# Nine more products of zeros on TensorE at the head of an attention and MLP kernel

## The chip, the cores and the metric

The kernel runs on one core of one Trainium2 chip. The time is device microseconds of one execution. Times before the change: 242.74, 243.67 and 244.24 us, median 243.67. One further execution was taken by the profiler; it is the one that the profile and the trace describe.

## The reference: what is computed

Four batches, eight heads, 768 rows, 64 columns a head. A small matrix of 8 x 8 for each batch and head, sort_net, is balanced by five rounds of softmax over rows and normalisation over columns. It then mixes the eight blocks of 96 rows of k and of v. Attention runs within blocks of 96 rows with the mixed keys and values, and a two-layer network with h * cos(h) follows.

```python
P = sort_net
for _ in range(5):
    P = np.exp(P - np.max(P, axis=-1, keepdims=True))
    P = P / (np.sum(P, axis=-1, keepdims=True) + 1e-09)
    P = P / (np.sum(P, axis=-2, keepdims=True) + 1e-09)
k_sorted = np.einsum('bhij,bhjcd->bhicd', P, k_b)
v_sorted = np.einsum('bhij,bhjcd->bhicd', P, v_b)
scores = scale * np.matmul(q_b, k_sb.transpose(0, 1, 2, 4, 3))
attn = softmax(scores)                  # rows of 96
x = np.matmul(attn, v_sb)               # then 3072 tokens x 512
h = x @ w_in                            # 512 -> 2048
out = (h * np.cos(h)) @ w_out           # 2048 -> 512
```

## The kernel before

The order of all work is written out by hand: each engine runs its instructions in the order in which the calls stand in the source, and waits where one needs another's result. Matrix inputs are converted to bf16 as they are loaded by POOL's DMA queue (q, k and v of batch 0 first, then w_in, w_out and the rest).

The tokens are cut into eight chunks n of four blocks (384 tokens), two chunks a batch. For a chunk the steps are: q transposed (q_turn, L301), scores qk (L422 for chunk 0, L427 for the others), row maximum and subtraction on VectorE (DVE; L482, L488), exp on ScalarE (ACT; L506), transposed p (p_transpose, L532, or a DMA), the product with v (av, L545) and its division (L552, L554), the transpose into xT (L572), then up (L585, cosine on ACT at L589, product on DVE at L592) and down (L609), and the store. The sorted keys come from ks (L360), the sorted values from vs (L450, L460). The parts of one chunk's attention are placed by hand between the up and down products of the chunk before; for chunk 0 there is no chunk before, so its attention stands alone, and its up runs in halves of two blocks: up(0, 0) to up(0, 7), first for the first two blocks.

The head of the kernel is this. POOL issues the loads of q, k and v of batch 0. DVE clears a tile `warm` of 128 x 128 zeros (L209). keep_warm(8) then gives TensorE (PE) eight products of that tile with a column of it, read 512 times; the result goes to a tile `idle` that nobody reads, and no engine waits for it. After that comes the balancing, which the code does for two groups g of two batches: maximum and exp (L240, L241), row sums through a product with a matrix of sums, sk (L262), and four rounds of exp on ACT (L331), sk on PE (L262), reciprocal, product and reciprocal on DVE (L350, L323, L326). PE's place between the rounds is filled: keep_warm(2) and keep_warm(3) after the first two sk, and the 32 transposes of q for chunk 0 (L301) in the later ones. In the second round a one-column copy on POOL, held (L346), waits for the balancing, and three loads of w_in (load_w_in, L158) are issued behind it. The balancing ends with spread(0), which writes bd (L282); the sorted keys of batch 0 (k_sort_0, L360, copied by DVE and ACT into kTs), a turn of bd (v_turn, L436), and the permutation of v on POOL (v_permute, L177, held behind bd by L354) follow. The second group's last step is done later, at L323 to L282 from last_balance().

The filler's own code, with the lines that follow it:

```python
def keep_warm(times):
    idle = big.tile([128, 512], FP32, name="idle", tag="big")
    for _ in range(times):
        nc.tensor.matmul(
            idle[:], warm[:], warm[:, :1].to_broadcast([128, 512]), start=True, stop=True)

keep_warm(8)
```

The rounds of the balancing:

```python
for it in range(4):
    for g in range(NG):
        nc.scalar.activation(E[g], T[g], AF.Exp, scale=ci[g][:])
    ...
    sk = [product(same, E[g]) for g in range(NG)]
    ...
    keep_warm(3 if it == 0 else 0)
```

Of the kernel before, what the change touches and what calls it, by code (L numbers as in the profile page):

```python
# [18 lines left out]
def kernel(  # L19
# [196 lines left out]
# [4 lines that stand above are left out]
            nc.tensor.matmul(  # L220
                idle[:], warm[:], warm[:, :1].to_broadcast([128, 512]), start=True, stop=True)

    keep_warm(8)


    E_eps = [const.tile([128, nb + 1], FP32, name=f"E{g}") for g in range(NG)]
# [717 lines left out]
```

## Time and profile before

| what | value |
|---|---|
| runs | 242.74, 243.67, 244.24 us |
| profiled execution, span from first to last instruction | 242.3 us |
| profiled execution, its time outside the span | not shown on the page |
| PE busy | 232.8 us (96%) |
| DVE, ACT, POOL busy | 173.7, 157.6, 88.2 us |
| chain that ended last | PE 83%, ACT 7%, DVE 4%, DMA 3% |
| of it, products of zeros L220 | 2.4% |
| HBM read, written | 27.27, 6.29 MB |

Times in the profile are microseconds from the start of the span. A row of the timeline gives start, duration, engine, line, operation, result and operands, shapes, the count of merged instructions, and in brackets the idle time ahead and what ended it. PE is the product, PEld the loading of the weights, which runs ahead of the products. A row of the chain gives start, duration and the engine's work to which that stretch of the end-to-end chain is put down. A row of the windows view gives a stretch, its length, the busy time (and instructions) of PE, PEld, DVE, ACT and POOL in it, the granted clock of PE, the share of the DMA engines and GB/s. Matmuls are pipelined and their ends are modelled, so a merged group of PE rows ends some time after its last product has been issued.

### The profile page before, as it was taken

What the parts mean: (1) busy time and instruction counts of PE and PEld (TensorE: products, weight loads), DVE (VectorE), ACT (ScalarE), POOL (GpSimd) and SP (SyncE); (2) the same over time, 40 slices, a digit from 0 to 9 for tenths busy, and PEclk for the clock granted to TensorE, in tenths of its full rate; (3) what the DMA queues carried; (4) which work ended last, traced back from release to release, by engine and by line L of the source; (5) the groups of instructions that cost most, each with busy time, mean ns of one, the idle gap of its engine ahead of it and who ended that gap; (6) DMA issues with size and microseconds to landing.
All of it is one profiled execution on the core that took longest, in us unless ns stands there. A gap on an engine that the chain in (4) does not pass through costs nothing.

```text
span 242.3 us, 5366 instructions
## 1 busy us (share of the span) xinstructions
PE 232.8 (96%) x2163; PEld 149.2 (62%) x2163; DVE 173.7 (72%) x320; ACT 157.6 (65%) x226; POOL 88.2 (36%) x110
## 2 busy tenths in 40 slices
PE   8979899899999999999999999999999999999994
PEld 3869798655666566655666556655565556456553
DVE  6469768996478965986669986898789769635700
ACT  4378866577488974889568957684568376737511
POOL 6469974399880899010535301700000000000000
PEclk9999999999999999999999999999999999999999
DMA  4999999991999958756789858914582460271012
GB/s 50 235 189 176 182 205 231 196 208 54 155 170 192 128 149 85 142 112 164 133 97 138 77 120 181 180 24 107 115 202 60 91 190 0 49 138 43 1 46 87
DMA packets 66681, 30.90 MB, mean 128 GB/s; under 512 B 55392, under 2 KB 62176, under 8 KB 66400
## 3 DMA queue, kind: packets, MB, share of 16 engines
q0 software_dynamic: 24048, 13.64, 40.8%
q1 hardware_dynamic: 42096, 16.72, 29.0%
q8 instruction: 17, 0.28, 0.5%
q10 hardware_dynamic: 512, 0.20, 0.3%
q14 instruction: 8, 0.07, 0.1%
HBM read 27.27 MB, written 6.29 MB: 139 GB/s over the span
## 4 chain that ended last, share of the span: by engine, by line
PE 83%; ACT 7%; DVE 4%; DMA 3%; issue 1%; ACTq 0%; DVEq 0%
PE h L585 33%; PE o L609 28%; PE sc L427 4%; PE av L545 3%; PE ks L360 3%; PE idle L220 2%; DMA vperm<-p_buf 2%; ACT p_buf L506 2%; PE xps L572 2%; PE sk L262 2%; PE vs L460 2%; DVE gg L592 1%; PE vs L450 1%; ACT kTs L288 1%; ACT vS L288 1%; PE pps L532 1%
## 5 line engine op out<-in xcount | busy, mean ns | idle before, releaser
L585 PE MATMUL h<-xT,w_in_t 128*128 128x384 bf16 (+1 forms) x576 | 93.0, 313 | 0.3 <-DVE gg L592 0.2
L609 PE MATMUL o<-w_out_t,gg 128*128 128x512 bf16 x368 | 88.3, 379 | 0.5 <-DVE s L488 0.5
L589 ACT ACTIVATE c<-h,half_pi 128x768 f32<-128x768 f32 (+1 forms) x72 | 59.8, 830 | 28.8 <-PE h L585 26.6
L592 DVE TENSOR_TENSOR gg<-c,h 128x768 bf16<-128x768 f32 (+1 forms) x72 | 61.2, 860 | 22.6 <-ACT c L589 22.6
L585 PEld LDWEIGHTS <-w_in_t 128*128 128x128 bf16 x576 | 53.8, 100 | 27.4 <-issue 1.0
L609 PEld LDWEIGHTS <-gg 128*128 128x128 bf16 x368 | 33.2, 98 | 31.9 <-DVE s L488 0.7
L482 DVE TENSOR_REDUCE mx<-sc 96x4 f32<-96x384 f32 (+1 forms) x43 | 31.9, 743 | 2.9 <-PE sc L427 1.7
L488 DVE TENSOR_TENSOR s<-sc,mx 96x384 f32<-96x384 f32 (+1 forms) x43 | 32.2, 749 | 2.3
L177 POOL COPY vperm<-kv 64x1536 bf16<-64x1536 bf16 (+1 forms) x10 | 28.0, 2837 | 12.1 <-DMA kv<-in_v_dram 12.1
L506 ACT ACTIVATE p_buf<-s 96x768 bf16<-96x768 f32 x32 | 25.9, 839 | 0.5 <-DVE s L488 0.2
L554 DVE TENSOR_TENSOR xn<-av,r 96x512 bf16<-96x512 f32 x32 | 22.0, 686 | 1.1
L427 PE MATMUL sc<-kTs,q_turned 128*128 128x96 bf16 x224 | 16.1, 206 | 0.7 <-DVE s L488 0.7
L134 POOL DMA_DIRECT2D kv<-in_q_dram x24 | 16.0, 688 | 0.7 <-issue 0.7
L552 DVE RECIPROCAL r<-av 96x8 f32<-96x8 f32 x32 | 6.4, 199 | 13.6 <-PE av L545 13.4
L427 PEld LDWEIGHTS <-q_turned 128*128 128x128 bf16 x224 | 12.9, 98 | 5.1 <-DVE s L488 1.3
L288 ACT COPY o_s<-o 128x512 f32<-128x512 f32 (+2 forms) x11 | 5.9, 538 | 15.4 <-PE o L609 9.1
L288 ACT CAST kTs<-ks 128x512 bf16<-128x512 f32 (+2 forms) x25 | 12.4, 497 | 4.8 <-PE ks L360 4.7
L288 ACT COPY kv<-o 128x512 f32<-128x512 f32 x8 | 4.7, 583 | 12.6 <-PE o L609 12.6
L134 POOL DMA_DIRECT2D q_mem<-in_q_dram x16 | 10.7, 685 | 0.3 <-issue 0.3
L589 ACT ACT_TABLE_LOAD x8 | 10.3, 1283 | 0.1
L288 ACT CAST pair<-vs 96x512 bf16<-96x512 f32 (+1 forms) x12 | 8.7, 729 | 2.0 <-PE vs L460 2.0
L288 ACT COPY xT<-xps 128x384 bf16<-128x384 bf16 (+1 forms) x9 | 4.6, 513 | 8.1 <-PE xps L572 8.1
(102 smaller groups left out, 226.7 us busy)
## 6 DMA issues: line engine op xcount, KB each, us to landing
out_dram<-kv SPq DMA_DIRECT2D x12, 256.0 KB, 3.0
out_dram<-o_s SPq DMA_DIRECT2D x11, 256.0 KB, 2.4
w_in_t<-in_moe_w_in_dram POOLq DMA_DIRECT2D x4, 512.0 KB, 10.5
w_out_t<-in_moe_w_out_dram POOLq DMA_DIRECT2D x4, 512.0 KB, 12.8
kv<-in_k_dram POOLq DMA_DIRECT2D x2, 768.0 KB, 13.4
kv<-in_v_dram POOLq DMA_DIRECT2D x2, 768.0 KB, 15.2
pair<-in_k_dram POOLq DMA_DIRECT2D x2, 768.0 KB, 11.7
kv<-in_v_dram POOLq DMA_DIRECT2D x6, 256.0 KB, 7.4
```

What stands on the lines that cost most here:

```text
L134: nc.gpsimd.dma_start(out=q_heads[:, i, :, e], in_=src[:, ih * IC + i, :, e])
L177: nc.gpsimd.tensor_copy(dst, src)
L288: eng.copy(dst, src)
L427: nc.tensor.matmul(out, q_of(n, hp)[:, x:x + 128], keys_of(n, u, h2, hp), start=True, stop=True)
L482: nc.vector.reduce_max(mx[:], scv, axis=AX.X)
L488: nc.vector.tensor_tensor(s, scv, mx.to_broadcast(list(s.shape)), op=ALU.subtract)
L506: nc.scalar.activation(p[:, :, :blk], s_t.pop((n, u)).rearrange("p e h c -> p (e h) c"), AF.Exp, scale=scale)
L554: nc.vector.tensor_tensor(xn.rearrange("p h e d -> p e h d"), avv[:, :, :, :D], r.to_broadcast([blk, 2, H2, D]), op=ALU.mult)
L585: nc.tensor.matmul(h[:, f2, :w], w_in_t[:, kk, f * 128:(f + 1) * 128], xT[n][:, kk, lo:hi], start=(kk == 0), stop=(kk == KC - 1))
L589: nc.scalar.activation(c[:, :, :w], h[:, :, :w], AF.Sin, bias=half_pi[:, 0:1])
L592: nc.vector.tensor_tensor(gt[n, fp][:, :, lo:hi], c[:, :, :w], h[:, :, :w], op=ALU.mult)
L609: nc.tensor.matmul(o[:], gt[n, f // 2][:, f % 2, ts * 128:(ts + 1) * 128], w_out_t[:, f, :], start=(f == 0), stop=(f == FC - 1))
```

## The change

The first call of keep_warm gives PE seventeen products of zeros in place of eight. The calls with two and three stay. On PE nine weight loads and nine products are added ahead of the first sk (L262); the instructions of the other engines and their order stay as they are.

```diff
@@ -220,7 +220,7 @@
             nc.tensor.matmul(
                 idle[:], warm[:], warm[:, :1].to_broadcast([128, 512]), start=True, stop=True)
 
-    keep_warm(8)
+    keep_warm(17)
```

## The prediction

> **What bounds the kernel now.** I read the page first: TensorE (PE) is busy 96% of the span, and its clock line shows full speed in every slice. That line is not to be taken at its word, so I went on to the chain of work that ended last, in order of time, where one form of instruction can be compared early and late.
>
> ```profile
> 1.04 3.60 PE idle L220 x8
> ...
> 27.77 0.50 PE xps L572 x4
> 28.27 0.64 PE pps L532 x8
> 28.92 1.36 PE h L585 x8
> 30.28 0.64 PE pps L532 x8
> 30.92 1.28 PE h L585 x8
> 32.20 0.47 PE av L545 x8
> 32.66 1.21 PE h L585 x8
> 33.87 0.89 PE ks L360 x32
> 34.76 0.36 PE av L545 x8
> 35.12 0.66 PE h L585 x8
> ...
> 79.84 1.73 PE o L609 x8
> ```
>
> Eight products h with 192 columns take 1.28 us at 30.92 and 1.21 at 32.66, but 0.66 us at 35.12; av falls from 0.47 to 0.36. So PE runs at half speed for the first 33 to 34 us and at full speed from there on. The windows view (clock: the figure before the last two) does not say it for the early stretch, but it does know a fall at the very end:
>
> ```profile
> 18.30:23.40 5.10, 5.10 (x80) 4.90 (x77) 5.00 (x6) 4.08 (x8) 5.10 (x6) 1.00 1.13 172
> 238.40:241.80 3.40, 0.32 (x3) 0.04 (x1) 0.29 (x1) 0.27 (x1) 0.00 (x0) 1.00 0.23 71
> 241.80:242.30 0.50, 0.00 (x0) 0.00 (x0) 0.00 (x0) 0.00 (x0) 0.00 (x0) 0.58 0.00 0
> ```
>
> The record evidently begins with its first switch. The last two rows show the clock falling to a mean of 0.58 over the last half microsecond; at half speed that is a fall at 241.9, 3.2 us after the last product (PE's 0.32 us from 238.40 on).
>
> What brought full speed? The chain shows PE going from product to product with no gap from 27.77 (each start is the start before plus its time) until the switch, some 6.0 us. The 3.60 us of zero products at the start did not do it.
>
> **The change, part by part.** Nine products and their weight loads are added on PE ahead of L262. Nothing else moves: every other engine keeps its order.
>
> (a) The zero products. At half speed each takes 0.427 us (3.4 us from the first to the first sk, by eight); at full speed one with 512 columns takes 1.73 / 8 = 0.216 us. Seventeen at half speed would be 7.26 us, until 8.30. The unknown is when PE switches: not before 3.6 us of products and, by the stretch from 27.77, at the latest after about 6.0 us, so between 4.64 and 7.1. I take the middle, 5.9: 11.4 products until then, 5.6 more at 0.216 us, end at 7.1. The ends give 6.5 and 7.7. The first sk starts at 4.43 now, so the balancing begins 2.7 us later (2.0 to 3.3).
>
> [...]
>
> (b) The balancing, from the first sk at 4.43 to bd's end at 13.43, 9.0 us.
>
> ```profile
> 4.43 1.03 PE L262 MATMUL sk<-maskj,L 128*128 128x8 f32 x4
> 5.85 1.03 PEld L262 LDWEIGHTS sk<-E,same 128*128 128x128 f32 x4 [0.44 <-ACT E L331]
> 6.12 0.86 PE L262 MATMUL sk<-E,same 128*128 128x8 f32 x4
> 7.73 1.10 PEld L262 LDWEIGHTS sk<-E,same 128*128 128x128 f32 x4 [0.37 <-ACT E L331]
> 8.06 0.86 PE L262 MATMUL sk<-E,same 128*128 128x8 f32 x4
> 9.67 1.21 PE L262 MATMUL sk<-E,same 128*128 128x8 f32 x4
> 10.30 0.21 DVE L350 RECIPROCAL rr<-sk 128x8 f32<-128x8 f32 x1 [0.47 <-PE sk L262]
> 13.08 0.35 DVE L282 SCALAR_TENSOR_TENSOR bd<-maskp,ci,T 128x128 bf16<-128x128 f32 x1
> ```
>
> Most of a round is DVE and ACT and stays. PE's part shrinks in two ways. The fillers (L220, and the transposes L301) now hold up sk: at 5.85 and 7.73 the weights load, and the product starts 0.27 and 0.33 us later, behind the fillers; at full speed two or three fillers take 0.43 or 0.65 us and are out of the way. That is 0.6 us. And the wait from sk's start to rr (9.67 to 10.30, about 0.6 us) comes five times; no row shows this fp32 form at full speed, so its gain lies between nothing and half, 0.3; I take 0.2, for h's products gain a third to a half: 1.0 us. Together 1.6 (0.6 to 2.1): bd ends 1.1 us later than now.
>
> (c) From bd to the first row maximum, 4.9 us.
>
> ```profile
> 13.48 0.58 PE L360 MATMUL ks<-bd,kv 64*128 64x32 bf16 x16 [0.37 <-DVE bd L282]
> 37.50 0.56 PE L360 MATMUL ks<-bd,kv 64*128 64x32 bf16 x16
> 8.85 0.85 PE L301 MATMUL qps<-ident,q_mem 96*64 96x96 bf16 x12
> 38.76 0.56 PE L301 MATMUL qps<-ident,q_mem 96*64 96x96 bf16 x16
> 17.77 0.80 PE L422 MATMUL sc<-kTs,q_turned 64*96 64x96 bf16 x15 [0.17 <-ACT kTs L288]
> 18.29 0.95 DVE L482 TENSOR_REDUCE mx<-sc 96x8 f32<-96x768 f32 x1 [1.21 <-PE sc L422]
> ```
>
> The key products with 32 columns gain nothing (0.58 and 0.56), the ACT and DVE copies of kTs stay; the scores with 96 columns gain about as the q transposes do (0.85 for twelve, 0.56 for sixteen), 0.25 us on the way to mx, and the end of the key products and of the turn of bd, each waited for once, perhaps 0.15. The maximum starts 0.7 us later than now.
>
> (d) 18.29 to 28.9: nothing. In the row 18.30:23.40 above DVE (the third busy time) works 5.00 of 5.10 us: it goes from maximum to subtraction without a pause, so a faster PE only waits for it. Only the last x transpose gains 0.15 us: up(0, 0) comes 0.5 us later.
>
> (e) The first halves of up(0), to the fifth of them.
>
> ```profile
> 28.81 1.28 ACT L589 ACT_TABLE_LOAD   x1
> 30.32 0.58 ACT L589 ACTIVATE c<-h,half_pi 128x384 f32<-128x384 f32 x1 [0.22 <-PE h L585]
> 30.95 0.80 ACT L288 COPY pT<-pps 96x768 bf16<-96x768 bf16 x1
> 31.99 0.67 PE L545 MATMUL av<-vS,pT 96*128 96x65 bf16 x8
> 35.80 1.60 PE L585 MATMUL h<-xT,w_in_t 128*128 128x192 bf16 x16
> ```
>
> PE alone would save 0.7 on each of three h, 0.25 on each pps, 0.1 on av: over 2.5 us. But av(0, 2) stands in PE's order behind the copy pT, and that behind the table load and the first cosine on ACT, which do not shrink: 1.28 + 0.58 + 0.80 us after the start. So av comes 0.25 us later instead of 0.5. From 31.99 to 35.80, 3.8 us, PE is the bound; at full speed av 0.36, h 0.66, ks 0.89, av 0.36 and h 0.66 are 2.9 us. The fifth up starts 0.25 - 0.9, some 0.7 us earlier; pieces that overlap (ks behind h) take it to 0.9. After it both kernels run at full speed, so this stays.
>
> Sum: +2.7 - 1.6 - 0.4 - 0.15 - 1.4 = -0.85, I take -0.9 us. The span becomes 241.4. The page gives the span alone, 242.3; the runs have a median of 243.67, 1.4 above, and spread over 1.5 us, so I subtract from the median: 242.8. Own range from the bounds of (a), 0.7 either way, and (b), -0.5 to +1.0: 241.6 to 243.8.
>
> Queues. POOL's hold at 7.73 sits in the balancing, so three loads of w_in are issued some 2 us later.
>
> ```profile
> 7.85 2.30 POOL L158 DMA_DIRECT2D w_in_t<-in_moe_w_in_dram  x3
> 14.58 5.48 POOL L177 COPY vperm<-kv 64x1536 bf16<-64x1536 bf16 x2 [0.81 <-DMA kv<-in_v_dram]
> w_in_t<-in_moe_w_in_dram POOLq DMA_DIRECT2D x4, 512.0 KB, 10.5
> ```
>
> That costs nothing: k and v are still landing until 14.58 on the same queue, and w_in, some 10.5 us after its issue, is read from 28.9 on. The permutation of v now waits for that load and not for bd, and starts 0.6 us later behind the later bd; its first reader comes later by as much. If this cover were gone, its 0.6 us would be what remains of (c).
>
> **The rivals.** (1) Full speed does not come or does not hold through the balancing: slower. For it speaks that PE counts as busy for all 5.10 us from 18.30 to 23.40 without a switch, and that the balancing is thin work, with L262 waiting on ACT each round. Against it: those 5.1 us are products with 64 rows only, the zero products are full ones without a gap, and after 34 us nothing but a rest of 3.2 us brought the clock down. If it never rises, 9 x 0.427 = 3.84 us stand ahead of the balancing and nothing on the chain waits for a load to absorb them: 247.5. If it falls again early in the balancing, (a) costs 2.7, (b) returns half, 0.8: 245.6. The point that decides: (a) grows by half of any lateness of the switch, so at a switch 1.8 us later, about 7.7, gain and loss are even.
>
> [...] The rows at 8.85 and 38.76 show transposes to run faster at full speed, not whether they hold it.
>
> (2) The gain is larger: switch at 4.64, the fp32 products at half their time, PE bound in (e) throughout: -0.7 - 0.5 - 0.6 more, down to 241.0. Against it the ACT rows of (e).
>
> (3) The gain is covered: ACT and DVE, not PE, also set the rate after 32 us, and (e) returns 0.5 instead of 1.4; no change, 243.7 to 244.5.
>
> **How the numbers follow.** Forecast 0.55 (242.8, own range 241.6 to 243.8), rival 1 0.20 (half at 245.6, half at 247.5), rival 2 0.12, rival 3 0.13. One per cent, 2.4 us, is about what a measurement of this kernel can tell from no change. Faster by over that: 0.15, most of rival 2 and the edge of the forecast. Slower: 0.17, rival 1 and a little of rival 3. Within: 0.68. The range 241.0 to 245.6 leaves out the worse half of rival 1 and tails.
>
> **What would show it.** After: the starts of L220 change from 0.43 to 0.22 us apart between 4.6 and 7.1; the first sk near 7.1; bd near 14.5; mx near 19.0; eight products h in some 0.7 us from the first on; the fifth up near 34.9. I am wrong if eight h still take 1.3 us, if sk starts after 8, or if up(0, 0) comes as early as 28.9.

## The result, and the profile after

The changed kernel is slower: 245.25 us median of 20 executions against 243.4 us of the kernel before, ratio 1.006 with a 95% interval of 1.0038 to 1.0082 (the ratio leaves disturbed executions out, the medians do not). The forecast was 242.8, faster by 0.4%. The profiled execution took 245.65 us with a span of 243.9 from first to last instruction, 1.6 us longer than the span before.

The clock line of the page, the same that read 9 in every slice before:

```profile
PEclk9955569999999999999999999999999999999999
```

Since the record begins with its first switch, this line now tells what it could not tell before: PE was at full speed early, and then fell back for some 24 us. The windows view, with the clock third from the right:

```profile
1.19:4.60 3.41, 3.41 (x9) 1.21 (x8) 2.19 (x12) 2.30 (x7) 3.41 (x8) 1.00 0.27 20
4.60:8.01 3.41, 3.22 (x19) 1.73 (x17) 1.24 (x11) 0.57 (x2) 0.09 (x1) 1.00 1.30 213
8.01:11.43 3.42, 2.63 (x24) 1.67 (x24) 2.19 (x17) 1.20 (x4) 2.24 (x4) 1.00 1.02 216
11.43:14.84 3.41, 3.04 (x38) 2.79 (x39) 1.90 (x13) 1.91 (x4) 0.38 (x2) 0.50 0.95 186
31.91:35.32 3.41, 3.41 (x39) 2.98 (x37) 1.90 (x4) 1.70 (x4) 2.74 (x2) 0.50 1.24 205
35.32:38.73 3.41, 3.41 (x68) 3.16 (x65) 2.72 (x7) 2.48 (x6) 1.59 (x4) 1.00 1.29 229
```

The 1.00 of the first row means only that the record has not begun: the products of zeros are 0.43 us apart there. The clock rose at 4.60, fell at 11.43 and rose again at 35.32, and these times lie on one grid of 3.413 us (two steps, then seven). It was not an accident of this execution: all twenty have a mean clock between 0.939 and 0.958.

The profiled execution of the kernel before, on the other hand, is not typical of it. 63 further executions of the kernel before were timed beside the experiments, with the mean clock of each. 45 of them have a mean of 0.944 to 0.958, as the changed kernel has; 17 have 0.998 to 1.000, as the profiled one (0.999); one has 0.986. In the changed kernel a mean of 0.950 is a rise in the head, a fall, and 24 us at half speed. Without any zeros at the head (an experiment below) none of twelve executions has a mean under 0.986. So, by their mean clock, eight zeros, too, raised the clock in 45 of the 63 executions, and it fell again; no trace of such an execution was kept. The median of the 45 is 243.25 us, that of the 17 is 244.39. Against the 45 the changed kernel takes 2.0 us more, and nine products at 0.216 us are 1.94: it pays for nine more products and gets back only what most executions had already. The places compared below come from one execution of the rarer kind.

The chain of work that ended last shows what that did.

```profile
1.04 5.60 PE idle L220 x17
7.26 0.31 ACT E L331
7.62 0.40 PE sk L262 x2
...
14.12 0.36 DVE bd L282
...
28.86 0.50 PE xps L572 x4
29.36 0.64 PE pps L532 x8
30.00 1.37 PE h L585 x8
...
33.75 1.28 PE h L585 x8
35.03 0.92 PE ks L360 x32
35.95 0.36 PE av L545 x8
36.32 0.66 PE h L585 x8
```

The first sk of a round now follows the exp on ACT directly (7.57 to 7.62) and takes 0.40 us; before, it waited for the fillers. But h of the first half again takes 1.37 and 1.28 us for eight products, as before, and 0.66 only from 36.32. In the timeline the five places of the prediction's sum stand at:

```profile
6.48 0.51 PE L262 MATMUL sk<-maskj,L 128*128 128x8 f32 x4
...
14.12 0.35 DVE L282 SCALAR_TENSOR_TENSOR bd<-maskp,ci,T 128x128 bf16<-128x128 f32 x1
...
19.34 0.95 DVE L482 TENSOR_REDUCE mx<-sc 96x8 f32<-96x768 f32 x1 [1.22 <-PE sc L422]
...
29.93 1.44 PE L585 MATMUL h<-xT,w_in_t 128*128 128x192 bf16 x8
...
36.99 1.58 PE L585 MATMUL h<-xT,w_in_t 128*128 128x192 bf16 x16
```

The first up of the kernel before:

```profile
28.84 1.44 PE L585 MATMUL h<-xT,w_in_t 128*128 128x192 bf16 x8
```

| place | before | after | later by |
|---|---|---|---|
| first sk | 4.43 | 6.48 | 2.05 |
| bd | 13.08 | 14.12 | 1.04 |
| first row maximum | 18.29 | 19.34 | 1.05 |
| first up | 28.84 | 29.93 | 1.09 |
| fifth up | 35.80 | 36.99 | 1.19 |
| end of span | 242.3 | 243.9 | 1.6 |

Against the profiled execution before, the balancing returns 1.0 of 2.05 us; after it nothing is returned. The lateness then stays at 1.15 to 1.2 us to 190 us. The last 0.4 us comes at 195. The chain of the kernel before goes there from down to up without a wait; that of the changed kernel has a transposing transfer of x between, which landed later. First before, then after:

```profile
194.34 0.86 PE o L609 x4
195.21 3.90 PE h L585 x24
```
```profile
192.14 4.31 DMA xT<-xn
196.59 4.06 PE h L585 x24
```

### The profile page after: what moved, and what is told of

Its sections match the earlier page's. It is cut to its first block, busy times and chain, and to the rows that moved or that the text cites. A ratio compares the mean times of both kernels' runs of the same rounds, so it can differ in the third digit from the quotient of the medians.

```text
span 243.9 us, 5384 instructions
## 1 busy us (share of the span) xinstructions
PE 233.2 (96%) x2172; PEld 148.4 (61%) x2172; DVE 173.8 (71%) x320; ACT 157.6 (65%) x226; POOL 88.0 (36%) x110
## 4 chain that ended last, share of the span: by engine, by line
PE 79%; ACT 7%; DVE 6%; DMA 5%; issue 1%; DVEq 0%; ACTq 0%
PE h L585 33%; PE o L609 26%; PE sc L427 3%; PE av L545 3%; PE ks L360 3%; PE idle L220 2%; DMA vperm<-p_buf 2%; DMA xT<-xn 2%; ACT p_buf L506 2%; PE xps L572 2%; PE vs L460 2%; DVE gg L592 1%; PE vs L450 1%; ACT kTs L288 1%; ACT vS L288 1%
## 5 line engine op out<-in xcount | busy, mean ns | idle before, releaser
L552 DVE RECIPROCAL r<-av 96x8 f32<-96x8 f32 x32 | 6.4, 199 | 13.7 <-PE av L545 13.5
```

## The experiments

Two theories stood against each other. A: the clock rises through the zeros but falls in the thin rounds of the balancing, and so the rest of chunk 0 up to the fifth up runs at half speed as before; had it held, the gain would have come. B: the clock behind the head is worth nothing, since ACT and DVE set the rate there, and the loss is only the later start.

**Fillers in the rounds.** Edit, beside seventeen at the head:

```diff
-        keep_warm(3 if it == 0 else 0)
+        keep_warm((5, 3, 3, 3)[it])
```

> Seventeen products of zeros as in the changed kernel, and more fillers in the balancing: 5, 3, 3, 3 products of zeros behind the four sk in place of 3, 0, 0, 0. Theory A (the clock rises during the seventeen products, but falls back in the thin rounds of the balancing, and the rest of chunk 0 runs at half speed again): the clock holds past the point where it fell, 11.4 us, to the end of the balancing; bd comes some 0.5 us earlier than the 14.1 us of the changed kernel; then it falls in the thin stretch of the sorted keys; time some 0.5 us under the changed kernel, about 244.7. Theory B (the clock after the head is worth nothing, because ACT and DVE set the rate; the loss is only the later start): the added fillers bring nothing, 245.2 or up to 0.5 more.

Measured: 245.34 us, ratio 1.0061 (1.0033 to 1.0088).

```profile
13.28:16.70 3.42, 3.25 (x54) 2.23 (x53) 1.85 (x11) 2.29 (x5) 1.32 (x2) 1.00 1.01 163
16.70:20.11 3.41, 1.95 (x46) 1.64 (x43) 2.35 (x8) 2.92 (x9) 3.41 (x2) 1.00 1.24 208
20.11:23.52 3.41, 3.41 (x51) 3.32 (x47) 3.34 (x4) 2.58 (x6) 3.41 (x5) 0.50 0.88 122
```

The clock held through the balancing and fell at 20.1, behind the sorted keys, in whose stretch the fall had been forecast. That the fall hangs on how much PE has to do is borne out: PE was busy 3.25 of 3.42 us in the step before 16.70, at whose end the clock held, and 1.95 of 3.41 in the next, at whose end it fell. In this execution the clock rose only at 6.46, so the first sk came at 7.39 and bd at 14.88, 0.8 us later than in the changed kernel and not 0.5 earlier. The time did not drop: full speed in the last half of the balancing alone brought nothing more (first sk to bd 7.49 us, against 7.64 in the changed kernel), and the last fillers held up the first sorted keys by 0.3 us (0.71 us from bd to ks, before 0.40).

**Fillers everywhere.** Edit, shortened, beside the last one, where `fill` gives PE products of zeros into the tile named:

```diff
+        fill(ps.rearrange("p t m -> p (t m)"), 2)     # k_sort_0
+        if b == 0: fill(ps.rearrange("p t n -> p (t n)"), 1)     # v_sort_b
+        if n == 0: fill(sc[:, 0], 1)     # qk_part
+        if (n, u) in ((0, 0), (0, 1)): fill(a[:, 0], 2)     # av
```

> As the run before, and fillers in chunk 0 as well, each written into a PSUM tile ahead of its real products: 2 ahead of each group of sorted keys, 1 ahead of each group of sorted values and of each group of scores, 2 ahead of the first two products with v. Theory A: full speed holds from the head up to the first up, eight products h take 0.66 us from the first on, and the time falls below the kernel before: 242.5 (241.8 to 243.4). Theory B: full speed changes nothing and the fillers are in the way: 245.3 to 246.5. If the clock falls all the same, 246 to 248, since each filler then takes 0.43 us.

Measured: 256.42 us, ratio 1.0483 (1.0428 to 1.0538). A miss for both: the clock held to 25.4 us, but each filler stood between the release of a PSUM tile and its real products, and the stretch from bd to the first up grew from 15.8 to 23.3 us. Its total says nothing on the worth of the clock.

**No zeros at the head.** Edit: the first keep_warm is left out.

> No products of zeros at the head at all. Theory A: the eight of the kernel before ended just when the first sk was ready, and did not raise the clock, so this is the kernel before, 243.4 within 0.4 us. Theory B: the same. A third case: without the eight the clock rises later than 33.7 us, or the rounds run slower: 0.5 to 1.5 us more.

Measured: 244.98 us, ratio 1.0036 (1.0002 to 1.007). In its profile the first sk starts at 4.59, when DVE's L is there, and the first up at 29.09, both 0.2 us later than with eight; the fifth up is 0.2 us earlier. So the eight hide behind DVE. What they bring is the rise: the mean clock of these twelve executions is 0.986 to 1.000, and their median of 244.98 us lies nearer to the 244.39 than to the 243.25 above, that is to those executions of the kernel before whose clock did not rise in the head either. The rest of its profiled span, 1.7 us over the kernel before, was lost at 84.65 to 87.94 in a wait for a transposing transfer of p; whether the missing zeros have to do with that wait stays open.

**Thirty-four.** Edit: keep_warm(34).

> Thirty-four products of zeros at the head. Both theories: the seventeen further ones run at full speed, 0.216 us each, so the first sk comes 3.7 us later than in the changed kernel, and nothing downstream takes any of it up: 248.9. If waits on loads behind the balancing take some of it up, 247 to 248.5.

Measured: 251.67 us, ratio 1.0312 (1.0268 to 1.0357).

```profile
0.34:3.76 3.42, 2.72 (x7) 1.01 (x8) 1.61 (x12) 1.49 (x3) 3.05 (x12) 1.00 0.05 4
7.17:10.58 3.41, 3.41 (x19) 1.71 (x17) 0.42 (x6) 0.03 (x1) 0.00 (x0) 1.00 1.08 227
10.58:14.00 3.42, 2.70 (x24) 1.70 (x23) 1.97 (x16) 1.45 (x5) 1.52 (x3) 1.00 0.84 176
14.00:17.41 3.41, 3.35 (x28) 2.98 (x28) 1.85 (x15) 1.59 (x4) 0.91 (x2) 0.50 1.02 143
```

The clock rose at 3.76 already, held as long as the zeros lasted, and fell at 14.00, at the end of the first step in which the balancing stood without them. The first sk came at 9.77, 3.3 us later than with seventeen; the first up was 3.3 us later too: downstream takes nothing up. The rest of the span was lost behind 80 us: against the kernel before the lateness goes from 4.3 to 5.7 us near 90 us and to 7.0 near 120, and at both places the chain waits for a transposing transfer of p, 4.1 and 4.7 us, where that of the kernel before does not.

**Thirteen.** Edit: keep_warm(13).

> Thirteen products at the head and nothing else. Theory A: the clock rises in the same way, the first sk comes 1.4 us later than in the kernel before, the balancing returns 1.0, the clock falls and the rest is as before: 244.0, 1.0 us under the changed kernel, for four products of 0.216 us less. If the clock does not rise with thirteen, 245.5.

Measured: 244.31 us, ratio 1.0013 (0.9971 to 1.0056), not to be told from the kernel before.

```profile
7.95:11.36 3.41, 2.56 (x33) 1.97 (x32) 2.18 (x18) 1.48 (x5) 2.42 (x4) 1.00 1.04 220
11.36:14.78 3.42, 3.14 (x54) 2.78 (x54) 2.05 (x11) 2.05 (x4) 0.28 (x2) 0.50 0.92 180
```

The first sk came 1.14 us later than before and the balancing returned 1.32, so bd stood at 12.90, 0.2 us earlier than before, although the clock fell at 11.36. Four products less than seventeen were worth 1.2 us at bd in these two executions. So the loss of the changed kernel is the part of the zeros that the balancing cannot return. All twelve executions have a mean clock of 0.944 to 0.958, so by it the clock rose in all twelve. Their median is 1.06 us above that of the 45 executions with eight zeros whose clock rose, and five products at 0.216 us are 1.08; the times spread from 242.95 to 251.45 us, so the closeness of the two may be chance.

**Zeros on half the rows.** Edit, beside seventeen at the head:

```diff
-                idle[:], warm[:], warm[:, :1].to_broadcast([128, 512]), start=True, stop=True)
+                idle[:], warm[:64], warm[:64, :1].to_broadcast([64, 512]), start=True, stop=True)
```

> Seventeen products at the head as in the changed kernel, but every product of zeros (those of the fillers in the balancing too) uses only 64 of the 128 rows. In the runs so far, stretches full of products with 64 rows (18 to 25 us) never raised the clock. Theory A (what raises it is the share of the array at work, rows times time, and 64 rows are half): the clock does not rise at the head, all seventeen take 0.43 us, the first sk comes at 8.3 us and nothing is returned in the balancing: 247.3 (246.8 to 248). Theory B (a gapless stretch of any products raises it): as the changed kernel, 245.0, first sk near 6.5.

Measured: 249.68 us, ratio 1.0256 (1.0202 to 1.0311).

```profile
1.04 7.43 PE L220 MATMUL idle<-warm 64*128 64x512 bf16 x17 [1.04 <-DVE warm L209]
8.40 1.02 PE L262 MATMUL sk<-maskj,L 128*128 128x8 f32 x4
9.35 1.03 PE L220 MATMUL idle<-warm 64*128 64x512 bf16 x2
9.50 0.73 ACT L331 ACTIVATE E<-T,ci 128x8 f32<-128x8 f32 x2 [5.21 <-DVE ci L279]
10.31 0.93 PEld L262 LDWEIGHTS sk<-E,same 128*128 128x128 f32 x4 [0.84 <-ACT E L331]
10.31 1.02 PE L262 MATMUL sk<-E,same 128*128 128x8 f32 x4
```

Seventeen products without a gap, 0.425 us apart to the last (it starts at 7.84), and no rise: the first sk came at 8.40 and the clock first rose at 36.96, as theory A has it. It is 2.4 us slower in all than that theory gave; 0.8 of it stands in the balancing (9.44 us from the first sk to bd, against 8.65), where sk's weight loads no longer ran ahead of the fillers: the first E is done near 9.8, but PEld starts at 10.31 together with PE (in the kernel before at 5.85, 0.05 us behind E). In the profiled execution, 248.70 us, no more is lost behind it: bd comes 4.8 us later than before and the span ends 4.6 us later. Why two of the four executions took 250.7 and 251.1 us stays open.

**Holding the clock with single fillers.** Edits: the rounds get 4, 2, 2, 2, and beside that the first three kernels, with 13, 17 and 8 at the head, get six calls, the last two, with 13 and 17, seven longer ones. The longer ones, shortened:

```diff
+    keep_warm(5)     # ahead of k_sort_0(40, 8, A, *C)
+    keep_warm(2)     # ahead of qk(0, 0)
+    keep_warm(2)     # behind each of qk(0, 1), qk(0, 2), qk(0, 3)
+    keep_warm(2)     # behind av(0, 0, True)
+    keep_warm(2)     # behind x_transpose(0, 0, V, *C)
```

> Thirteen products of zeros at the head, and single fillers where PE waits anyway up to the first up: 4, 2, 2, 2 in the rounds of the balancing, 3 ahead of the last group of sorted keys, 1 ahead of the scores, 1 behind two groups of sorted values, 1 behind the first product with v, 2 behind the first x transpose. Theory A (full speed is worth something once it lasts to the first up): the clock rises at some point from 3.8 to 6.5 us and holds; the first sk comes 1.4 us later than in the kernel before, the balancing returns 1.0, keys and scores 0.3, the halves of up 1.0 to 1.5; time 242.5 (241.8 to 243.4). Theory B (ACT and DVE cover it): nothing is returned behind the balancing, 244.0 to 244.8.

> The same fillers with seventeen products at the head. Theory A: some 0.8 us behind the run with thirteen, 243.3, and 1.5 to 2 us ahead of the changed kernel, whose clock falls. Theory B: the changed kernel's 245.0 or, with the fillers, up to 0.5 more.

> The eight products of the kernel before, with the fillers. If eight do not raise the clock, each filler costs 0.43 us where PE has no room, and the time is 244 to 245.5. If they raise it in some executions (in the run with thirty-four the clock rose at 3.76 us, after 2.7 us of products), the times fall into two groups, the lower near 241.5.

> Thirteen products at the head, and fillers placed so that every stretch of 3.4 us up to the first up has at least a third of the array at work: 4, 2, 2, 2 in the balancing, 5 ahead of the last group of sorted keys, 2 ahead of the scores, 2 behind each of the last three groups of scores, 2 behind the first product with v, 2 behind the first x transpose. Theory A: the clock does not fall any more, eight products h take 0.66 us from the first on, the distance from the first up to the fifth shrinks from 7.0 to 5.6 us, and the time is 243.0 (242.0 to 244.0), the fillers giving back up to 0.8 us of that gain. Theory B (ACT covers it): the distance stays above 6.5 us and the time is over 244.5.

> The same fillers with seventeen products at the head. Theory A: as the run with thirteen, with the first sk 0.8 us later: 243.8 (242.8 to 244.6), so under the changed kernel by the 1.0 to 1.4 us that full speed in the halves of up is worth. Theory B: 245 or more.

Measured, in this order: 245.98 us (ratio 1.0083, 1.0047 to 1.0119), 247.78 (1.0167, 1.0099 to 1.0235), 245.83 (1.0069, 1.0018 to 1.0119), 247.78 (1.0170, 1.0140 to 1.0200), 248.45 (1.0178, 1.0145 to 1.0211). As kernels all five are misses. In none of the profiled executions did the clock hold to the first up: it fell at 18.8, 17.7, 21.3 and 24.1 us. With eight it did not rise at the head in the profiled execution; six of its twelve times lie at 243.6 to 244.6 us with a mean clock of 0.965 to 0.972, six at 247.1 to 248.2 with 0.997 to 1.000: the two groups expected, at other places. Behind the fall a filler costs 0.43 us (two took 0.85 us of the chain at 31.30 in the last of the five). But the second rise then came at very different distances from the first up, and that answers the question of A and B. The kernel with thirteen and the longer fillers, where full speed came back at 31.53:

```profile
31.23 0.95 PE L585 MATMUL h<-xT,w_in_t 128*128 128x192 bf16 x8
32.02 0.52 PE L532 MATMUL pps<-ident,p_buf 96*96 96x96 bf16 x8
32.38 0.83 PE L585 MATMUL h<-xT,w_in_t 128*128 128x192 bf16 x8
...
36.83 1.37 PE L585 MATMUL h<-xT,w_in_t 128*128 128x192 bf16 x13
```

From the first up to the fifth it takes 36.83 - 31.23 = 5.60 us, before 6.96. All profiles together, by how long after the first up full speed came:

| full speed after first up, us | first to fifth up, us | kernel |
|---|---|---|
| 5.39 | 7.06 | after |
| 4.82 | 6.96 | before |
| 4.64 | 6.87 | 34 zeros |
| 3.87 | 6.50 | no zeros |
| 3.34 | 6.30 | 17 on 64 rows |
| 3.18 | 6.27 | 13 zeros |
| 3.16 | 6.27 | fillers in rounds |
| 2.24 | 5.98 | 13 and fillers |
| 1.26 | 5.79 | 17 and longer fillers |
| 1.08 | 5.70 | 8 and fillers |
| 0.39 | 5.60 | 17 and fillers |
| 0.30 | 5.60 | 13 and longer fillers |
| 1.77 ahead of it | 5.60 | fillers everywhere |

The distance follows the clock from end to end, by 1.4 us. Theory B falls: ACT does not cover the halves of up. Shown is the worth of the clock for this stretch and, by the 1.1 us between the two kinds of execution of the kernel before, for a rise that lasts only into the balancing. A time below that of the kernel before is not shown: no version that was run beats it. One execution of the last kernel, its fastest by 1.5 us (246.40), has a mean clock of 0.997 against 0.976 to 0.979 of the other five, so there the clock may have held from the head on; no trace of it was kept, and it too is above the kernel before.

## Why the prediction was wrong

The step that failed is what (c), (d) and (e) take for granted, (e) in the words "at full speed av 0.36, h 0.66, ks 0.89, av 0.36 and h 0.66": that a clock once raised stays up to the first halves of up. It fell at 11.43, 6.8 us after it had risen and before the balancing was over, and the three terms, together -1.95 us, measured +0.15. The sign of being wrong that the prediction named, eight h still at 1.3 us, is what the trace shows. The first rival had this mechanism ("it falls again early in the balancing", 245.6) and had a tenth of the chance. Whether transposes hold full speed, which the prediction leaves open at its rows of 8.85 and 38.76, stays open: no run shows them by themselves.

The argument against that rival was that after 34 us nothing but a rest of 3.2 us brought the clock down. That was a reading of the stage where PE is never thin, carried to a stage where it is. The trace of before held the warning: in each round of the balancing ACT waits 0.85 to 1.22 us for DVE, and PE for ACT. What the runs show in its place can be worked out from the product records. Take for each product its columns at 0.427 us for 512 (0.216 at full speed), times its rows over 128, and add this up over the steps of the grid, here in the first 100 us of all thirteen profiles. In the ten steps at whose end the clock fell, the share lies between 0.16 and 0.36, in the changed kernel's step from 8.01 to 11.43 at 0.31. Of some 280 steps that held, all but two lie at 0.38 or above (the two, both 0.32, are from the run with fillers everywhere, and some records can be missing). The 23 steps that raised the clock lie at 0.73 and above, and none of some 70 that left it low is above 0.77. The rows matter: without them, steps between 20 and 28 us, full of products with 64 rows, would count over 0.9 and ought to have raised it. This is an estimate worked out from the product records of these thirteen profiles, and no more; one run, that with 64 rows, was made to test it.

A second premise failed beside it. The sum sets the changed kernel against a head at half speed, which the profiled execution had, and is then taken off the median of three other executions; most executions of that kernel, by their mean clock, had full speed in the balancing already. That "the 3.60 us of zero products at the start did not do it" holds for the profiled execution: by this count, the two steps of the grid in which its eight zeros lie have a share of 0.57 and 0.70, and no step under 0.73 raised the clock. So the -1.0 us of (b) that was measured in the profiles is no gain over most executions.

Point by point:

- (a), +2.7 us: the zeros cost 2.05. The mechanism was right, within its bounds of 2.0 to 3.3. The clock rose at 4.60, at the early end, which is luck of the grid: in the other kernels with seventeen on 128 rows at the head it rose between 4.08 and 7.04. That 6.0 us without a gap were needed before was, by the count, a misreading: that stretch began within a step of the grid, and the step from 26.84 to 30.25 has a share of 0.70, the next one, at whose end the clock rose, 0.93.
- (b), -1.6: measured -1.01 in the changed kernel, -1.14 to -1.37 where thirteen products at the head, or seventeen and more fillers behind them, stood, within the bounds of 0.6 to 2.1. Both parts are there: sk starts when ACT is done (7.62), and the two products of one sk take 0.40 us in the chain at full speed.
- (c), -0.4: +0.01, since the clock had fallen. The run with fillers in the rounds had full speed there, and took the same 5.22 us from bd to the maximum although fillers held up its first keys by 0.3 us. The run with thirteen and single fillers had full speed there too and took 4.95, 0.26 less. So full speed returns about 0.3 of the 0.4 us.
- (d), -0.15: +0.04, at half speed; how much full speed would return there was not measured without fillers.
- (e), -1.4: +0.10, since the clock was down. Its price was right: 6.96 to 5.60 us is 1.36, as the table shows.
- The loads, issued later behind POOL's hold, cost nothing that the trace shows: the lateness is 1.1 us at the first up and 1.2 at 190 us. Not forecast was that a transposing transfer of x lands later against the work around it, 0.4 us here.
- The break-even, a switch at 7.7, was worked out for a clock that stays. With one that falls, as here, the balancing alone pays, about 1.0 to 1.35 us, so against a head at half speed the zeros may delay the first sk by no more than that; thirteen do by 1.1 and come out even at bd, seventeen by 2.05 and lose. Against a head that eight zeros have raised already, the further ones are lost, as the 2.0 us of the changed kernel show.
- The upper end of the prediction's own range, 243.8, leaves out the 0.7 of (a) that the lower end has; with it the sum gives 244.5. Neither end allows for (c) to (e) falling out, which is what came.

## What to carry to other kernels

The products of zeros bought full speed here only for as long as the work behind them kept the array busy: 6.8 us in the changed kernel, 13.7 with fillers in the rounds. So look at the thinnest 3.4 us behind a warm-up before you pay for a longer one, and weigh products by rows as well as by time (seventeen on 64 rows did not raise the clock). One profile shows one phase of the grid: the profile of the kernel before has a mean clock of 0.999, and 45 of its 63 further executions have 0.944 to 0.958, so compare the mean clock of many executions with that of the profiled one before you take its head for the kernel's. Judge the clock in the first microseconds by the spacing of one form of product: the record read 1.00 there while the zeros were 0.43 us apart. If the clock will fall anyway, the warm-up may cost no more than the stage right behind it returns, here 1.0 to 1.35 us.

## What the runs showed of the hardware

- In the thirteen profiles the rises and falls of the clock lie whole steps of 3.413 us apart (4.60, 11.43 and 35.32 us in the changed kernel, two steps and seven). The phase of this grid against the kernel's start differs from profile to profile: the first rise came at 3.76, 4.08, 4.22, 4.54, 4.60, 4.94, 5.12, 6.46 and 7.04 us in the nine in which the clock rose at the head.
- In the run with thirty-four zeros, 2.7 us of full products in a step of 3.41 us raised it (rise at 3.76). By the mean clock eight products, 3.6 us, raised it in 45 of 63 executions. It fell without a rest of PE: in the changed kernel at the end of a step in which PE was busy 2.63 of 3.42 us, a share of the array of 0.31 by the count above; that count gives up to 0.36 for the ten steps that ended in a fall.
- Seventeen gapless products on 64 rows, 7.3 us, did not raise it (first rise at 36.96 us; mean clock 0.999 to 1.000 in all four executions); on 128 rows seventeen did in all twenty executions of the changed kernel, by their mean clock of 0.939 to 0.958.
- Sixteen products with 32 columns took 0.58 us at half speed (at 13.48 us in the kernel before) and 0.56 us at full speed (at 37.50).
